# Two attention layers and two FFT convolutions on one core: the residual loaded early, an eight-slot spectrum ring, column-half stores, and twiddles read over dead keys and weights

## The chip, the cores and the metric

The kernel runs on one core of one Trainium2 chip. The metric is the time of one execution in device microseconds (us). Every run below lists its median and, where there were rounds, the ratio to the kernel before, executed in turn with it on the same chip. In the traces, times count from the first instruction of the execution. PE is TensorE, DVE is VectorE, ACT is ScalarE, SP is the engine whose queue issues nearly all transfers (55.46 of the 56.41 MB).

## The reference

Four layers, each added to the residual x: a sliding attention with eight dilated positions, a convolution with a kernel generated from a state-space model and applied by FFT, and both once more.

```python
def _A_ref(x, wqkv, wo):                      # B=1, S=2048, D=512, 32 heads of 16
    W, dil = 8, 2
    q, k, v = split((x @ wqkv))               # cut: reshapes
    idx = pos[:, None] - arange(W)[None, :] * dil      # 8 positions back, step 2
    logits = einsum("bhsd,bhswd->bhsw", q, k[idx]) * Dh ** -0.5   # masked where idx < 0
    return einsum("bhsw,bhswd->bhsd", softmax(logits), v[idx]) @ wo

def _B_ref(u, A, B, C, log_dt, Dskip):        # L=2048, D=512, N=128
    K = einsum("dn,dnl,dn->dl", C, exp(dt * A * l), dt * B).real  # the convolution kernel
    y = irfft(rfft(u, 2L) * rfft(K, 2L))[:L]                      # cut: padding
    return y + u * Dskip

x = A_x
for _ in range(2):
    x = x + _A_ref(layernorm(x), A_wqkv, A_wo)
    x = x + _B_ref(layernorm(x), ...)         # the same weights both times
```

## The kernel before

In an attention core the work goes in this order: for each query block q and feature tile ft, DVE multiplies queries by shifted keys (`prod`), PE sums the products over the features of a head, DVE takes the row maximum (`mx`), ACT the exponentials, DVE normalises. Meanwhile PE makes the v rows. Every four v rows, two copies shift them by one position for the dilated window, and an event may issue other work. Then come sixteen value multiplies (`pav`), each summed by PE and projected, with further events at their places. Engine order is fixed by the program here.

```python
def v_proj(a):
    ...                                                       # cut: matmuls, ACT copy into v
    if a % 4 == 3:                                            # one v block is complete
        b = a // 4
        nc.sync.dma_start(v[1:113, s0:s1, :], v[0:112, s0 + 16:s1 + 16, :])
        nc.sync.dma_start(v[113:128, s0:s1, :], v[112:127, s0 + 16:s1 + 16, :])
        event(("v", b))

for q, ft in slots:
    mult(q, ft); proj(per)                                    # product; projections in between
    if ft == 0 and q > 0: mx(q - 1)
    lsum(q, ft)
    if ft == 0 and q > 0: sub_exp(q - 1)
    if ft == 2 and q > 0: norm_p(q - 1)                       # cut: details
for n in range(16):
    ...; pv_mult(n); ...; event(("p", n)); pv_sum(n)
    if n > 0: out_proj(n - 1)                                 # adds the residual x_sb

ev = {("v", 1): [lambda: k_half_load(0)], ("v", 3): [x_load],
      ("p", 0): [G(gx, 0)], ("p", 1): [G(gw, 0), G(gs, 0), G(gx, 1)], ...,  # inverse twiddle
      ("p", 6): [lambda: k_half_fix(0), K(0, 0)], ("p", 7): [K(0, 1)], ("p", 8): [K(0, 2)],
      ("p", 9): [K(0, 3), lambda: k_half_load(1)], ...}       # kernel rows, in two halves
```

`k_half_load` is 18 small loads of one half of the convolution kernel's rows, in the SP queue; `K(h, j)` copies a quarter of a half into the FFT's order. There is one row buffer, so the second half is loaded only when the first is copied.

The convolution's middle stage (`u_f2`, then `i1`) multiplies each spectrum piece by the kernel's spectrum out of a ring of four slots, and feeds the inverse transform:

```python
def consume(p2, ec):
    kc = self.kf_ring[:, self.nkf % 4]; self.nkf += 1
    for h in range(2):
        nc.sync.dma_start(self.kf_ring[h::2, (self.nkf - 1) % 4], self.kf_dram[g, ec])
    nc.scalar.copy(ub[:], p2...)
    nc.vector.tensor_tensor(t1[...], ub[:], kc[:, 0], ALU.mult)
    nc.vector.tensor_tensor(t2[...], ub[:], kc[:, 1], ALU.mult)
```

## Time and profile before

| | before |
|---|---|
| median of 3 runs | 529.23 us (528.22 to 531.11) |
| span of the profiled run | 525.7 us, granted PE clock 0.933 |
| first product of the first core, first value multiply | 132.72, 171.90 |
| layer norm that closes the first layer (first `ln_bn<-pq`) | 233.46 |
| same for the second layer | 452.22 |
| last convolution's multiply stage, first to last | 467.57 to 500.65 |

A timeline line reads: start, duration, engine, source line, operation, output and inputs, count, and in brackets the idle time just before and what ended it. The prediction below shows the lines of the kernel before that carry it.

### The profile page before, as it was taken

How to read it: one execution, taken by the hardware profiler on the slowest of the kernel's cores; microseconds unless marked ns; L12 is line 12 of the kernel's file. 1: busy time of each engine (PE TensorE's matmuls, PEld its weight loads, DVE VectorE, ACT ScalarE, POOL GpSimd, SP SyncE). 2: the span in 40 equal slices, each digit the busy share in tenths (PEclk: the TensorE clock that was granted, in tenths of full speed). 3: DMA queues.
4: the chain of work that ended last, by engine and by line, in shares of the span. 5: the costliest groups of instructions: out<-in, count | busy, mean ns of one | idle time of the engine just before them, and what ended most of it. 6: DMA issues, size and time to landing. Idle time of an engine off the chain costs nothing.

```text
span 525.7 us, 12773 instructions
## 1 busy us (share of the span) xinstructions
PE 373.4 (71%) x5489; PEld 280.5 (53%) x5528; DVE 421.7 (80%) x570; ACT 330.4 (63%) x529; POOL 44.0 (8%) x56
## 2 busy tenths in 40 slices
PE   1000528899797797888866596889989998695595
PEld 1000225666453665667756485445556776485584
DVE  7799979998796998877679846828999988396843
ACT  5999597764353497788658534674444576695532
POOL 2000131010000002230000000200000013300000
PEclk9999969999797799998989979899998999997889
DMA  8803401011146410328768621161130130218403
GB/s 226 323 1 42 78 1 42 7 22 43 22 119 162 164 42 21 82 88 345 250 205 270 213 82 51 31 247 74 53 90 1 44 120 1 81 52 308 125 2 160
DMA packets 50043, 56.41 MB, mean 107 GB/s; under 512 B 28617, under 2 KB 37962, under 8 KB 48706
## 3 DMA queue, kind: packets, MB, share of 16 engines
q1 hardware_dynamic: 49842, 55.46, 33.1%
q8 instruction: 43, 0.70, 0.6%
q10 hardware_dynamic: 144, 0.13, 0.1%
q14 instruction: 14, 0.11, 0.1%
HBM read 38.67 MB, written 13.24 MB: 99 GB/s over the span
## 4 chain that ended last, share of the span: by engine, by line
PE 37%; DVE 24%; ACT 18%; DMA 7%; issue 6%; SPq 5%; POOL 2%; POOLq 0%; DVEq 0%; ACTq 0%
DVE pav L342 6%; PE pp L201 5%; PE pq L294 4%; PE pq L142 4%; PE pk L961 3%; SPq L1031 3%; PE pb L648 3%; PE pb L698 3%; PE pb L699 3%; PE L L252 3%; PE po L350 2%; DVE t L683 2%; DVE prod L245 2%; DVE t L684 2%; DMA kf_ring<-kf_dram 2%
## 5 line engine op out<-in xcount | busy, mean ns | idle before, releaser
L342 DVE TENSOR_TENSOR pav<-attn,v_ext 128x4096 bf16<-128x4096 bf16 x32 | 72.8, 2282 | 5.3 <-DMA x_sb<-in_A_x_dram 5.3
L350 PE MATMUL po<-ident,pav 128*128 128x128 bf16 x1024 | 64.4, 223 | 15.8 <-DVE pav L342 15.8
L350 PEld LDWEIGHTS <-pav 128*128 128x128 bf16 x1024 | 60.8, 100 | 26.0 <-DVE pav L342 22.9
L245 DVE TENSOR_TENSOR prod<-qT,kT_ext 128x4096 bf16<-128x4096 bf16 x29 | 65.6, 2285 | 5.7 <-PE L L252 4.8
L698 PE MATMUL pb<-Wp,t 128*128 128x128 bf16 x256 | 36.8, 238 | 20.7 <-DVE t L683 18.0
L682 ACT CAST ub<-pb 128x1024 bf16<-128x1024 f32 x32 | 32.1, 1025 | 10.8 <-DVE t L684 9.6
L201 PE MATMUL pp<-xnT,wqk 128*128 128x512 bf16 x123 | 31.9, 397 | 7.8 <-ACT xnT L194 7.1
L698 PEld LDWEIGHTS <-t 128*128 128x128 bf16 x256 | 27.3, 108 | 18.7 <-DVE t L683 18.6
L637 ACT CAST a1s<-pb 128x1024 bf16<-128x1024 f32 x30 | 30.1, 1017 | 10.2 <-PE pb L648 9.2
L296 ACT CAST v_ext<-pq 128x512 bf16<-128x512 f32 x32 | 18.7, 586 | 27.7 <-PE pq L294 27.7
L699 PE MATMUL pb<-WpJ,t 128*128 128x128 bf16 x256 | 35.9, 238 | 0.2 <-DVE t L684 0.2
L192 PE MATMUL pt<-ident,x_blk 128*128 128x128 bf16 x64 | 5.6, 241 | 41.4 <-ACT x_blk L118 41.4
L252 PEld LDWEIGHTS <-prod 128*128 128x128 bf16 x928 | 27.2, 97 | 14.6 <-DVE prod L245 9.4
L657 PE MATMUL pb<-a1s,w_sb 128*128 128x64 bf16 x768 | 30.7, 196 | 6.0 <-DVE a1s L637 2.5
L961 PE MATMUL pk<-B_t,A_t 128*64 128x84 bf16 (+1 forms) x512 | 25.2, 210 | 12.4 <-POOL ln_rstd L100 9.1
L294 PE MATMUL pq<-wv,xnT 128*128 128x512 bf16 x120 | 32.4, 398 | 0.6 <-issue 0.2
L353 ACT CAST oT<-po 128x512 bf16<-128x512 f32 x32 | 18.5, 579 | 22.8 <-PE po L350 22.5
L142 PE MATMUL pq<-xnT,wqk 128*128 128x512 bf16 x118 | 31.3, 391 | 1.6 <-issue 0.8
L252 PE MATMUL L<-ind,prod 128*128 128x8 bf16 x928 | 27.7, 166 | 6.2 <-DVE prod L245 6.0
L100 POOL TENSOR_SCALAR ln_rstd<-ln_veps 128x4 f32<-128x4 f32 (+1 forms) x11 | 15.1, 1370 | 203.1 <-DVE ln_veps L98 203.1
L657 PEld LDWEIGHTS <-w_sb 128*128 128x128 bf16 x768 | 27.1, 100 | 8.8 <-issue 3.9
L961 PEld LDWEIGHTS <-A_t 128*64 128x64 bf16 (+1 forms) x512 | 23.0, 110 | 15.7 <-POOL ln_rstd L100 9.6
(204 smaller groups left out, 913.5 us busy)
## 6 DMA issues: line engine op xcount, KB each, us to landing
kf_ring<-kf_dram SPq DMA_DIRECT2D x64, 256.0 KB
w_sb<-w_dram SPq DMA_DIRECT2D x8, 1024.0 KB
w_dram<-w_zero SPq DMA_DIRECT2D x1, 4096.0 KB
kf_dram<-kf_sb SPq DMA_DIRECT2D x16, 256.0 KB
v_ext<-v_ext SPq DMA_DIRECT2D x6, 448.0 KB
x_blk<-in_A_x_dram SPq DMA_DIRECT2D x4, 512.0 KB
wqk<-in_A_wqkv_dram SPq DMA_DIRECT2D x4, 512.0 KB
x_sb<-in_A_x_dram SPq DMA_DIRECT2D x4, 512.0 KB
```

The lines of the kernel that those rows point to most:

```text
L142: nc.tensor.matmul(pq[:], lhsT=self.wqk[:, dt, ft * P:(ft + 1) * P], rhs=self.xnT[:, dt, q * 512:(q + 1) * 512], start=(dt == 0), stop=(dt ...
L201: nc.tensor.matmul(pp[:], lhsT=self.wqk[:, dt, D + ft * P: D + (ft + 1) * P], rhs=self.xnT[:, dt, b * 512:(b + 1) * 512], start=(dt == 0), ...
L245: nc.vector.tensor_tensor(pr, self.qT[q][:, ft].unsqueeze(1).to_broadcast([P, W, 4, P]), kap, ALU.mult)
L252: self.nc.tensor.matmul(L[:, al, w, ft * 8:(ft + 1) * 8], lhsT=pr[:, w, al, :], rhs=self.c["ind8"][:], start=False, stop=True, skip_group_ ...
L294: nc.tensor.matmul(pp[:], lhsT=xnT[:, dt, a * P:(a + 1) * P], rhs=wv[:, dt, :], start=(dt == 0), stop=(dt == NDT - 1))
L342: nc.vector.tensor_tensor(pv[:], attn[:, n % 4].unsqueeze(2).to_broadcast([P, W, DH, H]), vap, ALU.mult)
L350: nc.tensor.matmul(po[:, ft, :], lhsT=pvf[:, w, ft * P:(ft + 1) * P], rhs=ident[:], start=(w == 0 and ft == 0), stop=(w == W - 1), skip_gr ...
L657: nc.tensor.matmul(p2[:, j, :], lhsT=self.w2[:, ec * EC + j, :], rhs=a1s[:, ec * EC + j, :], start=True, stop=True)
L682: nc.scalar.copy(ub[:], p2[:].rearrange("p e q -> p q e"))
L698: nc.tensor.matmul(p3[:, j, :], lhsT=t1[:, dql, :], rhs=wp_r, start=True, stop=False)
L699: nc.tensor.matmul(p3[:, j, :], lhsT=t2[:, dql, :], rhs=wpj_r, start=False, stop=True)
L961: nc.tensor.matmul(o, lhsT=lhs, rhs=Bt[:, ri, c * CH + ql].rearrange("p b g -> p (b g)"), start=(not half and j % 4 == 0 and ri == 0), sto ...
```

## The change

The intent: take the 18 small loads from in front of the last v shift by issuing them behind it and the residual early; open the pool of products first, so that it doesn't wait for a spare tile; normalise one product later; free space for four more ring slots in the last convolution, by loading the 4 MB forward twiddle over the dead keys and weights; and store the output in column halves, so that half of it leaves a stage sooner.

```diff
-        self.wqk = self.keep.tile([P, NDT, 2 * D], BF16, name="wqk")
-        self.kT = self.keep.tile([P, NDT, NA + 14, P], BF16, name="kT_ext")
+        slot = self.keep.tile([...], BF16, name="kT_ext", tag="slot")   # wqk and kT are views of it
+            self.prp = c2.enter_context(tc.tile_pool(name=f"a{l}_prod", ...))   # now first
             big = c2.enter_context(...)
...
-            self.prp = c2.enter_context(tc.tile_pool(name=f"a{l}_prod", ...))
-                if ft == 2 and q > 0:
+                if ft == 3 and q > 0:
                     norm_p(q - 1)
+    def load_w2(self, w2_dram):
+        w2 = self.keep.tile([P, P * P], BF16, name="w2_sb", tag="slot")
+        ...                                                   # four loads of 1 MB
-        w2p = ... ; self.w2 = w2p.tile(...); 4 x dma_start    # was in FftB.open_mid
+        self.ring2 = (second tile of four slots) if t else None
-            kc = self.kf_ring[:, self.nkf % 4]
+            ring, slot = self.kf_ring[self.nkf // 4 % len(self.kf_ring)], self.nkf % 4
-        ev = {("v", 1): [lambda: k_half_load(0)], ("v", 3): [x_load],
+        ev = {("v", 0): [x_load], ("v", 3): [lambda: k_half_load(0)],
-              ... ("p", 8): [K(0, 2)], ...
+              ... ("p", 8): [lambda: la.load_w2(w2_dram), K(0, 2)], ...
-        la.core(x_sb, u)
+        la.core(x_sb, u, {("p", 8): [lambda: la.load_w2(w2_dram)]})
-    zip_run(fb.i1(1), fb.i2(0, None), lead=2)
-    zip_run(fb.i2(1, <store of 4 full rows>, ("act", "dve")))
+    zip_run(fb.i1(1), fb.i2(0, store(0)), lead=2)             # column half 0 leaves here
+    zip_run(fb.i2(1, store(1), ("act", "dve", "act", "both")))
```

Cut: the pools' closing, and a mask moved into another tile.

More of the change, by code (lines that the diff above doesn't have):

```diff
@@ L129, in __init__ @@
         self.keep = self.ctx.enter_context(tc.tile_pool(name=f"a{layer}_keep", bufs=1, side="right"))
-        self.wqk = self.keep.tile([P, NDT, 2 * D], BF16, name="wqk")
+        slot = self.keep.tile([P, NDT * (2 * D + (NA + 14) * P)], BF16, name="kT_ext", tag="slot")
+        self.wqk = slot[:, 0:NDT * 2 * D].rearrange("p (t c) -> p t c", t=NDT)
         self.wsrc = A_wqkv.rearrange("(dt p) c -> p dt c", p=P)
         self.A_wo = A_wo
-        self.kT = self.keep.tile([P, NDT, NA + 14, P], BF16, name="kT_ext")
+        self.kT = slot[:, NDT * 2 * D:].rearrange("p (t a q) -> p t a q", t=NDT, q=P)
         self.xnT = xnT
@@ L224, in open_logits @@
     def open_logits(self):
-        self.ps_l = self.ctx.enter_context(self.tc.tile_pool(name=f"a{self.layer}_ps_l", bufs=2, space=PSUM, side="right"))
+        self.lctx = ExitStack()
+        self.ps_l = self.lctx.enter_context(self.tc.tile_pool(name=f"a{self.layer}_ps_l", bufs=2, space=PSUM, side="right"))
         self.st = [dict() for _ in range(4)]
@@ L270, in core @@
         with ExitStack() as c2:
+            self.prp = c2.enter_context(tc.tile_pool(name=f"a{l}_prod", bufs=2, reuse_waits="tile"))
             big = c2.enter_context(tc.tile_pool(name=f"a{l}_big", bufs=1, reuse_waits="tile"))
@@ L277, in core @@
             wk = c2.enter_context(tc.tile_pool(name=f"a{l}_wk", bufs=2, reuse_waits="tile"))
-            self.prp = c2.enter_context(tc.tile_pool(name=f"a{l}_prod", bufs=2, reuse_waits="tile"))
             pavp = c2.enter_context(tc.tile_pool(name=f"a{l}_pav", bufs=2, reuse_waits="tile"))
@@ L457, in core, with close_logits @@
             u_apply(14, range(14, 16))
+    def load_w2(self, w2_dram):
+        w2 = self.keep.tile([P, P * P], BF16, name="w2_sb", tag="slot")
+        self.w2 = w2[:].rearrange("p (e c) -> p e c", c=P)
+        for c in range(4):
+            self.nc.sync.dma_start(self.w2[:, c * 32:(c + 1) * 32, :], w2_dram[:, c * 32:(c + 1) * 32, :])
+    def close_logits(self):
+        self.lctx.close()
     def close(self):
@@ L492, in build_b_consts @@
     pf = pk[:, 7:8]
-    aux = cpool.tile([P, 4], F32, name="aux")
+    aux = cpool.tile([P, 8], F32, name="aux")
     nc.vector.tensor_tensor(aux[:, 0:1], pk[:, 6:7], rik, ALU.add)
@@ L497, in build_b_consts @@
     bk, p21 = aux[:, 0:1], aux[:, 1:2]
-    dmask_m = cpool.tile([P, 4], F32, name="dmask_m")
-    nc.vector.tensor_scalar(dmask_m[:], d4i[:], d4m, 2.0 / 4096.0, ALU.is_equal, ALU.mult)
+    dmask_m = aux[:, 4:8]
+    nc.vector.tensor_scalar(dmask_m, d4i[:], d4m, 2.0 / 4096.0, ALU.is_equal, ALU.mult)
     def off_cols(name, rcol, v00, v10, v01, v11):
@@ L555, in build_b_consts @@
         nc.vector.tensor_tensor(w[:], ws[name][:].unsqueeze(2).to_broadcast([P, 32, 4]),
-                                dmask_m[:].unsqueeze(1).to_broadcast([P, 32, 4]), ALU.mult)
+                                dmask_m.unsqueeze(1).to_broadcast([P, 32, 4]), ALU.mult)
         C[name] = w
@@ L614, in open_mid @@
         tc, nc, t = self.tc, self.nc, self.tag
-        w2p = self.c_mid.enter_context(tc.tile_pool(name=f"b{t}_w2", bufs=1, reuse_waits="tile"))
-        self.w2 = w2p.tile([P, P, P], BF16, name="w2_sb")
-        for c in range(4):
-            nc.sync.dma_start(self.w2[:, c * 32:(c + 1) * 32, :], self.w2_dram[:, c * 32:(c + 1) * 32, :])
         nc.sync.dma_start(self.g2[:], self.g2_dram[:])
@@ L622, in open_mid @@
             self.ring_pool = self.c_mid.enter_context(tc.tile_pool(name=f"b{t}_kf", bufs=1, reuse_waits="tile"))
+        self.ring2 = self.c_mid.enter_context(tc.tile_pool(name=f"b{t}_kf2", bufs=1, reuse_waits="tile")) if t else None
         self.nkf = 0
@@ L670, in u_f2 @@
         if self.kf_ring is None:
-            self.kf_ring = self.ring_pool.tile([P, 4, 2, DQG, EC], BF16, name="kf_ring", tag="kp")
+            self.kf_ring = [self.ring_pool.tile([P, 4, 2, DQG, EC], BF16, name="kf_ring", tag="kp")]
+            if self.ring2 is not None:
+                self.kf_ring.append(self.ring2.tile([P, 4, 2, DQG, EC], BF16, name="kf_ring2"))
         t1 = self.gtile("t1", [P, DQG, P])
@@ L676, in consume @@
         def consume(p2, ec):
-            kc = self.kf_ring[:, self.nkf % 4]
+            ring, slot = self.kf_ring[self.nkf // 4 % len(self.kf_ring)], self.nkf % 4
+            kc = ring[:, slot]
             self.nkf += 1
             for h in range(2):
-                nc.sync.dma_start(self.kf_ring[h::2, (self.nkf - 1) % 4], self.kf_dram[g, ec])
+                nc.sync.dma_start(ring[h::2, slot], self.kf_dram[g, ec])
             ub = self.wk.tile([P, DQG, EC], BF16, name="ub")
@@ L714, in i2 @@
                 nc.tensor.matmul(p4[:, j, :], lhsT=self.g2[:, 1, a, :], rhs=z[:, NA + a, :], start=False, stop=True)
-            self.evac(x_sb[:, t * 4:t * 4 + 4, dsl], p4[:], pat[t % len(pat)])
+            if pat[t % len(pat)] == "both":
+                self.evac(x_sb[:, t * 4:t * 4 + 2, dsl], p4[:, 0:2], "act")
+                self.evac(x_sb[:, t * 4 + 2:t * 4 + 4, dsl], p4[:, 2:4], "dve")
+            else:
+                self.evac(x_sb[:, t * 4:t * 4 + 4, dsl], p4[:], pat[t % len(pat)])
             if rows_done is not None:
@@ L1114 @@
         K = lambda h, j: lambda: k_part(h, j)
-        ev = {("v", 1): [lambda: k_half_load(0)], ("v", 3): [x_load],
+        ev = {("v", 0): [x_load], ("v", 3): [lambda: k_half_load(0)],
               ("p", 0): [G(gx, 0)], ("p", 1): [G(gw, 0), G(gs, 0), G(gx, 1)],
               ("p", 3): [G(gw, 1), G(gs, 1), G(gx, 2)], ("p", 4): [G(gw, 2), G(gs, 2), G(gx, 3)], ("p", 5): [G(gw, 3), G(gs, 3)],
-              ("p", 6): [lambda: k_half_fix(0), K(0, 0)], ("p", 7): [K(0, 1)], ("p", 8): [K(0, 2)], ("p", 9): [K(0, 3), lambda: k_half_load(1)],
+              ("p", 6): [lambda: k_half_fix(0), K(0, 0)], ("p", 7): [K(0, 1)], ("p", 8): [lambda: la.load_w2(w2_dram), K(0, 2)], ("p", 9): [K(0, 3), lambda: k_half_load(1)],
               ("p", 12): [lambda: k_half_fix(1), K(1, 0)], ("p", 13): [K(1, 1), K(1, 2)], ("p", 14): [K(1, 3)]}
@@ L1121 @@
     krctx2.close()
-    la.close()
+    la.close_logits()
     z0 = xnT[:].rearrange("p t c -> p (t c)").rearrange("p (m c) -> p m c", m=2 * NA)
     fb = FftB(tc, nc, C, consts["ident"], w2_dram, g2_dram, kf_dram, x_sb, 0)
-    fb.z0, fb.ring_pool = z0, kpp
+    fb.z0, fb.ring_pool, fb.w2 = z0, kpp, la.w2
     fb.open_mid()
@@ L1133 @@
     fb.c_mid.close()
+    la.close()
     la = LayerA(tc, nc, consts, lnst, A_wqkv, A_wo, 1, xnT, 1)
@@ L1150 @@
     with tc.manual_schedule(engines={ET.DVE, ET.Activation, ET.PE, ET.SP}):
-        la.core(x_sb, u)
-    la.close()
+        la.core(x_sb, u, {("p", 8): [lambda: la.load_w2(w2_dram)]})
+    la.close_logits()
     fb = FftB(tc, nc, C, consts["ident"], w2_dram, g2_dram, kf_dram, x_sb, 1)
-    fb.z0, fb.ring_pool = z0, None
+    fb.z0, fb.ring_pool, fb.w2 = z0, None, la.w2
     fb.open_mid()
@@ L1160, with store, rows @@
     fb.c_mid.close()
+    la.close()
     out_v = out.rearrange("b (p a) d -> p (b a) d", p=P)
-    zip_run(fb.i1(1), fb.i2(0, None), lead=2)
-    zip_run(fb.i2(1, lambda t: nc.sync.dma_start(out_v[:, t * 4:(t + 1) * 4, :], x_sb[:, t * 4:(t + 1) * 4, :]), ("act", "dve")))
+    def store(g):
+        gs = slice(g * 4 * DQG, (g + 1) * 4 * DQG)
+        def rows(t):
+            for a in ((t * 4, t * 4 + 2) if (g, t) == (1, 3) else (t * 4,)):
+                a1 = a + (2 if (g, t) == (1, 3) else 4)
+                nc.sync.dma_start(out_v[:, a:a1, gs], x_sb[:, a:a1, gs])
+        return rows
+    zip_run(fb.i1(1), fb.i2(0, store(0)), lead=2)
+    zip_run(fb.i2(1, store(1), ("act", "dve", "act", "both")))
     fb.c_ps.close()
```

## The prediction

> **What bounds the kernel now.** I read the page first, then each engine's timeline around the waits that the change touches, then the queue's timeline. The page says that no engine is the bound for the whole run:
>
> ```profile
> PE 373.4 (71%) x5489; PEld 280.5 (53%) x5528; DVE 421.7 (80%) x570; ACT 330.4 (63%) x529; POOL 44.0 (8%) x56
> ```
>
> DVE carries most, so gaps in DVE that end in something the change removes are what it can win. The first two are in the first attention layer. DVE's timeline (start, duration, and in brackets the idle time before and what ended it):
>
> ```profile
> 128.55 0.71 DVE L210 COPY kT_ext<-kT_ext 128x508 bf16<-128x508 bf16 x1
> 132.72 4.49 DVE L245 TENSOR_TENSOR prod<-qT,kT_ext 128x4096 bf16<-128x4096 bf16 x2 [3.46 <-PE L L252]
> ...
> 165.35 1.22 DVE L307 TENSOR_REDUCE mx<-L 128x128 bf16<-128x1024 f32 x1
> 171.90 4.49 DVE L342 TENSOR_TENSOR pav<-attn,v_ext 128x4096 bf16<-128x4096 bf16 x2 [5.33 <-DMA x_sb<-in_A_x_dram]
> ```
>
> The 5.33 us is blamed on the residual load, but the multiply reads v_ext. The queue in that time shows what it waited for:
>
> ```profile
> 154.54 9.55 SPq L1031 DMA_DIRECT2D k_rl<-kd_dram  x17
> 164.20 0.57 SPq L300 DMA_DIRECT2D v_ext<-v_ext  x1
> 164.82 0.88 SPq L301 DMA_DIRECT2D v_ext<-v_ext  x1
> 165.80 0.87 SPq L300 DMA_DIRECT2D v_ext<-v_ext  x1
> 166.71 0.83 SPq L301 DMA_DIRECT2D v_ext<-v_ext  x1
> 167.58 2.19 SPq L1109 DMA_DIRECT2D x_sb<-in_A_x_dram  x4
> ```
>
> The last v row block left ACT at 162.24 (161.66 + 0.58), yet its two shifting copies are issued only at 165.80, behind 18 small loads of the convolution kernel (0.80 + 9.55 us), and the 2 MB residual then shares the engines with them.
>
> The third place is the last convolution. DVE and the queue:
>
> ```profile
> 477.66 0.68 DVE L684 TENSOR_TENSOR t<-ub,kf_ring 128x1024 bf16<-128x1024 bf16 x1
> 479.90 0.69 DVE L683 TENSOR_TENSOR t<-ub,kf_ring 128x1024 bf16<-128x1024 bf16 x1 [1.56 <-DMA kf_ring<-kf_dram]
> ...
> 485.31 1.23 DVE L637 CAST xnT<-pb 128x1024 bf16<-128x1024 f32 x1 [2.89 <-PE pb L699]
> ...
> 488.39 1.23 DVE L637 CAST xnT<-pb 128x1024 bf16<-128x1024 f32 x1 [0.65 <-PE pb L699]
> ...
> 492.25 1.22 DVE L637 CAST xnT<-pb 128x1024 bf16<-128x1024 f32 x1 [1.44 <-PE pb L699]
> ```
>
> The eighth spectrum multiply waits 1.56 us for its ring slot (four slots), and DVE then idles 2.89 + 0.65 + 1.44 us for inverse-transform tiles that PE could start only after that multiply. After the last tile DVE alone finishes four multiplies while PE waits (PE idle 5.5 us until the multiply of L683).
>
> Fourth, the twiddle loads (4 MB each) and the end:
>
> ```profile
> 232.42 2.04 SPq L618 DMA_DIRECT2D w_sb<-w_dram  x4
> ...
> 517.82 4.26 SPq L1163 DMA_DIRECT2D out_dram<-x_sb  x4
> 520.50 1.22 DVE L637 CAST x_sb<-pb 128x1024 bf16<-128x1024 f32 x1 [1.29 <-PE pb L714]
> ```
>
> [...] from 154 to 164 us the queue issues without a gap (0.56 us each) while the engines average a share of 0.49, 0.18 and 0.54 in the three 4 us windows from 154. [...] PE stops at 163.9, the clock falls from about 165.5; it is 0.50 from 166 to 178 around the first stall and from 480 to 485 after PE's wait in the last convolution. [...]
>
> **The change, part by part.**
>
> *First attention layer.* (a) The pool of products is opened first. In the built program the first product of the core now waits for the last kernel-table matmuls (done at 128.5) and no longer for the L252 sums that read the spare tile in its place. It can start when DVE is free, 128.55 + 0.71 = 129.3 instead of 132.7. PE gains less: its next sums stood idle from 132.7 to 135.07, 2.4 us, and from there PE has no gap over 0.6 us until 164. So the projections, with the last v block, come 2.4 us earlier: ACT finishes it at about 159.8. (b) The normalisation moves one product later; this hides its 1.94 us wait for the exponentials, worth nothing by itself as PE sets the pace here. I stepped DVE through the new order with the two product buffers: the product for block 3 starts when its query arrives (163.1 - 2.4 = 160.7), ends at 162.9, the maximum (1.15) at 164.0. (c) The residual is issued after the first v shift and the kernel loads after the last one, so the last shift is issued at 159.9 and 160.5. In layer 2, where nothing stands in front, the second was issued at 390.37 and landed 3.2 us on (the chain of waits). Here: 163.7, up to 164.5 as the 2 MB residual precedes it. The value multiplies start at 164.0 to 164.5 instead of 171.9: **7.5 us**. From there DVE is nearly full (idle under 1 us in 172 to 200 us), so the gain stays. The kernel loads now run from 161 to 172, well before their first use at 199.8 - 7.5.
>
> *Twiddle over the dead keys, first convolution.* The load moves from 232.4 to about 190 (after the last product, 197.4 - 7.5). At the 426 GB/s seen from 236 to 244 it takes 4.2 MB / 0.426 = 9.8 us, done near 201; the second kernel load starts near 203, so they hardly meet. Its first use, the forward matmuls of L657, is at 245.2, and none of those waited for the load. **0**, perhaps 0.5 less contention.
>
> *Twiddle, second convolution.* It was already loaded at 345.5; now it is at about 417, done at 427, used at 465 in the old clock. **0**. What it buys is space: the rings of the last convolution (8 slots, 16 loads) are filled near 330 to 350, where the queue is free.
>
> *Ring of eight.* All of group 0 is resident, so 1.56 us go. More: the scheduler, seeing no ring wait, now places multiplies 10 and 11 ahead of the first DVE evacuation of the inverse tiles, and leaves two multiplies instead of four for after the last one. I stepped this with the trace's durations (multiply pair 1.20, evacuation 1.14 on DVE; ScalarE 0.92; inverse tile 1.0 us on PE, 1.75 at half clock; four PSUM buffers, three copies). Multiply 8 starts at 478.3. With PE at half clock until about 484, the gaps shrink to 0.95 + 0.6 + 0.45 and the stage ends at 495.8 against 500.65; with a warm PE at 493.8. I take **5.0 us**.
>
> *Stores.* Half of the 2 MB goes out during the stage before, in 512 B rows. The last evacuation is split, but the built program makes the DVE half wait for the ACT half[...]. What remains is the last transfer: 128 KB instead of 512 KB, at 0.4 MB per us 0.33 against 1.28 us (379 and 408 GB/s are seen at the end), less one extra issue of 0.34. **0.6 us.**
>
> Sum: 7.5 + 0 + 0 + 5.0 + 0.6 = 13.1; 529.2 - 13.1 = 516.1, I say 516.
>
> **The rivals.** First, *a new wait takes the place*: the shifts land late behind the residual, since 4 x 512 KB now go ahead of three of the four shifts. The engines ran at 1.0 share with 270 GB/s when they met in the run before. Against it: the residual has 8 us of lead. If the last shift still landed at 167, the first part would be 5 and the total 518.5. Second, *the last convolution is bound by the PE clock, not by the ring*: then only the 1.56 us come off and the total is 519.5. For it: the longest of its gaps (2.89) lies in the half-clock stretch. Against: DVE has multiplies to fill it. Third, *the gain of the first layer is lost to the first convolution*, whose spectrum stores make DVE wait 4.6 us for DMA: this stage follows no fixed clock and only moves along. A mild form, the new order of stores and ring loads, may cost or save 1 us. Fourth, the whole is better than stepped: PE stays warm, 514.
>
> **Range and chances.** The first layer is good to about 1 us, the ring to 2 (1.6 to 7), the rest to 1.5. That gives 511.5 to 521. 2% faster is 518.6; it takes one rival nearly whole to miss it: faster 0.78, same 0.21, slower 0.01.
>
> **What would show it.** In the changed profile: the first product at 129 to 130; the first value multiply near 164 with under 1 us of idle; the queue's v shifts directly after the v rows; no DVE wait for the ring in the last convolution, and its multiply stage under 29 us from first to last (33.1 before); twiddle loads near 190 and 410 without a waiter; a tail from the last matmul of 4.6 us or less (5.2 before). I would be wrong if the first value multiply still waits over 3 us for DMA, if the gaps of the last convolution only change their name, or if a kernel-row fix in the first layer starts to wait for its load.

## The result

The changed kernel took a median of **522.44 us** (520.3 to 523.23, 4 runs) against 528.98 us (528.22 to 531.11, 4 runs): ratio **0.9864** (95% interval 0.9821 to 0.9907). A later run of the same kernel on another chip (after_again, below) gave 0.9793 (0.9742 to 0.9844). A ratio here is the mean time of one kernel's fast runs over that of the other's of the same rounds, so not quite the ratio of the medians quoted. The prediction of 516.0 was too fast by 6.4 us and its range, 511.5 to 521.0, missed the median by 1.4.

The profiled run spans 518.5 us (clock 0.936). No engine's load changed, as the engine line of its page says:

```profile
PE 374.9 (72%) x5489; PEld 283.3 (55%) x5528; DVE 421.4 (81%) x570; ACT 330.0 (64%) x530; POOL 44.1 (9%) x56
```

DVE's timeline of the changed kernel in the first layer, the places shown before:

```profile
128.61 0.72 DVE L211 COPY kT_ext<-kT_ext 128x508 bf16<-128x508 bf16 x1
129.43 4.49 DVE L247 TENSOR_TENSOR prod<-qT,kT_ext 128x4096 bf16<-128x4096 bf16 x2
...
160.68 1.22 DVE L309 TENSOR_REDUCE mx<-L 128x128 bf16<-128x1024 f32 x1
168.38 4.49 DVE L344 TENSOR_TENSOR pav<-attn,v_ext 128x4096 bf16<-128x4096 bf16 x2 [6.48 <-DMA k_rl<-kd_dram]
...
223.14 0.43 DVE L1119 COPY k_perm<-k_rl 128x1024 bf16<-128x1024 bf16 x1 [1.68 <-DMA k_rl<-kd_dram]
...
232.05 0.70 DVE L75 BATCH_NORM_STATS2 ln_bn<-pq 128x6 f32<-128x512 f32 x1 [3.38 <-PE pq L364]
```

The first product comes 3.3 us earlier, and DVE is ready for the value multiplies at 161.9 instead of 166.6. But the wait before them has grown from 5.33 to 6.48 us, and a new wait of 1.68 us stands before a copy of the kernel rows. The queue in the same time:

```profile
151.71 1.96 SPq L1124 DMA_DIRECT2D x_sb<-in_A_x_dram  x4
153.78 0.60 SPq L302 DMA_DIRECT2D v_ext<-v_ext  x1
...
157.53 0.53 SPq L302 DMA_DIRECT2D v_ext<-v_ext  x1
158.10 1.47 SPq L303 DMA_DIRECT2D v_ext<-v_ext  x1
159.61 1.35 SPq L1030 DMA_DIRECT2D k_rl<-kd_dram  x1
162.17 12.81 SPq L1046 DMA_DIRECT2D k_rl<-kd_dram  x17
```

The last shift is issued at 158.1 instead of 166.7, 8.6 us sooner, yet the multiply that reads it starts only 3.5 us sooner. In the last convolution the wait on the ring is gone, and the three gaps before the inverse tiles have shrunk from 2.89 + 0.65 + 1.44 to 0.33 + 0.36 + 0.29:

```profile
482.72 1.23 DVE L645 CAST xnT<-pb 128x1024 bf16<-128x1024 f32 x1 [0.33 <-PE pb L710]
...
485.51 1.22 DVE L645 CAST xnT<-pb 128x1024 bf16<-128x1024 f32 x1 [0.36 <-PE pb L710]
...
488.23 1.23 DVE L645 CAST xnT<-pb 128x1024 bf16<-128x1024 f32 x1 [0.29 <-PE pb L710]
```

To see where the time went I cut every trace at the same seven places of DVE's timeline. A: from the end of DVE's last key copy to the first value multiply. B: to the layer norm that closes the first layer. C: to the last spectrum multiply of the first convolution. D: to the layer norm that closes the second layer. E: to the first spectrum multiply of the last convolution. F: to the end of its last multiply. G: to the end. All in us; the start, some 129 to 131 us, is left out. It is the same work in all of these kernels and differs by up to 1.5 us between executions.

| kernel (fast profiled runs) | A | B | C | D | E | F | G |
|---|---|---|---|---|---|---|---|
| before | 42.6 | 61.6 | 69.4 | 149.3 | 15.4 | 33.1 | 25.1 |
| changed | 39.1 | 63.7 | 68.1 | 150.5 | 16.2 | 27.4 | 24.3 |
| resid_behind | 32.5 | 65.7 | 69.0 | 150.6 | 16.2 | 27.4 | 26.0 |
| krows_behind | 38.5 | 67.0 | 68.4 | 149.9 | 15.2 | 26.2 | 25.6 |
| shifts_alone | 32.5 | 66.4 | 68.5 | 149.9 | 15.2 | 26.2 | 25.6 |
| w2_behind | 41.6 | 62.5 | 68.4 | 149.9 | 15.2 | 26.2 | 25.4 |
| norm_back | 41.3 | 61.9 | 70.5 | 149.3 | 16.1 | 26.2 | 24.6 |
| ring_four | 39.0 | 63.8 | 71.3 | 150.0 | 15.3 | 32.8 | 25.5 |
| pool_back2 | 39.0 | 64.4 | 67.9 | 150.0 | 16.3 | 27.5 | 24.4 |
| before_order | 38.9 | 64.2 | 69.1 | 149.4 | 15.5 | 32.1 | 24.8 |
| rb_sooner | 32.5 | 63.0 | 67.8 | 150.7 | 16.2 | 27.5 | 24.1 |
| rb_gs | 34.3 | 62.8 | 68.3 | 150.0 | 15.3 | 26.2 | 25.7 |
| resid_first | 35.6 | 63.3 | 68.5 | 151.7 | 16.1 | 26.2 | 24.4 |
| joined | 32.5 | 61.6 | 71.0 | 149.3 | 16.1 | 26.2 | 24.5 |
| combo1, the same kernel | 32.5 | 61.4 | 69.0 | 150.7 | 16.3 | 27.5 | 24.2 |

Before to changed: A -3.6, B +2.1, C -1.4, D +1.2, E +0.8, F -5.7, G -0.7; with the start's +0.1 that is the span's -7.2. The first layer, A + B, was to give 7.5 and gave 1.5. C varies by 3.5 us between kernels that do the same there (2.0 between joined and combo1, which are one kernel), E has two values, 15.2 to 15.5 and 16.1 to 16.3, and F and G partly trade against each other (27.4 + 24.3 and 26.2 + 25.5 are the same 51.7; with eight slots the sum runs from 50.6 to 53.4). Differences of that size in one execution are not explained below. A and B trade too: norm_back, whose first layer is the changed kernel's, has A 2.3 longer and B 1.8 shorter than the changed kernel, and no wait on the kernel rows. So a difference of 2 us in B alone means something only where A is equal, and A + B (102.7 and 103.2 in these two) is the safer figure.

### The profile page after: what moved, and what is told of

It reads as the page before. It is cut to its first block, busy times and chain, and to the rows that moved or that the text cites.

```text
span 518.5 us, 12773 instructions
## 1 busy us (share of the span) xinstructions
PE 374.9 (72%) x5489; PEld 283.3 (55%) x5528; DVE 421.4 (81%) x570; ACT 330.0 (64%) x530; POOL 44.1 (9%) x56
## 4 chain that ended last, share of the span: by engine, by line
PE 39%; DVE 22%; ACT 20%; DMA 8%; issue 5%; SPq 3%; POOL 2%; POOLq 0%; DVEq 0%; ACTq 0%
PE pp L202 5%; DVE pav L344 5%; PE po L352 4%; PE pq L143 4%; PE pk L976 3%; PE pb L709 3%; PE pq L296 3%; DMA v_ext<-v_ext 3%; PE pb L710 3%; PE pb L656 3%; PE L L254 3%; DVE prod L247 3%; DMA kf_dram<-kf_sb 2%; DVE t L694 2%; ACT ws L894 2%
## 5 line engine op out<-in xcount | busy, mean ns | idle before, releaser
L352 PE MATMUL po<-ident,pav 128*128 128x128 bf16 x1024 | 67.0, 228 | 14.7 <-DVE pav L344 14.5
L352 PEld LDWEIGHTS <-pav 128*128 128x128 bf16 x1024 | 63.3, 103 | 25.3 <-DVE pav L344 22.1
L202 PE MATMUL pp<-xnT,kT_ext 128*128 128x512 bf16 x123 | 31.9, 396 | 7.7 <-ACT xnT L195 7.0
L693 ACT CAST ub<-pb 128x1024 bf16<-128x1024 f32 x32 | 32.1, 1034 | 6.7 <-DVE t L695 5.9
L355 ACT CAST oT<-po 128x512 bf16<-128x512 f32 x32 | 18.5, 578 | 25.4 <-PE po L352 25.4
L665 PEld LDWEIGHTS <-w_sb 128*128 128x128 bf16 x768 | 28.3, 102 | 9.1 <-DVE a1s L645 3.9
L143 PE MATMUL pq<-xnT,kT_ext 128*128 128x512 bf16 x118 | 31.3, 392 | 1.6 <-issue 0.8
L364 PE MATMUL pq<-wop,oT 128*128 128x512 bf16 x112 | 29.7, 379 | 2.5 <-ACT oT L355 1.7
L254 PE MATMUL L<-ind,prod 128*128 128x8 bf16 x928 | 27.5, 166 | 4.9 <-DVE prod L247 4.7
```

Source lines behind the costliest of these rows:

```text
L143: nc.tensor.matmul(pq[:], lhsT=self.wqk[:, dt, ft * P:(ft + 1) * P], rhs=self.xnT[:, dt, q * 512:(q + 1) * 512], start=(dt == 0), stop=(dt ...
L202: nc.tensor.matmul(pp[:], lhsT=self.wqk[:, dt, D + ft * P: D + (ft + 1) * P], rhs=self.xnT[:, dt, b * 512:(b + 1) * 512], start=(dt == 0), ...
L254: self.nc.tensor.matmul(L[:, al, w, ft * 8:(ft + 1) * 8], lhsT=pr[:, w, al, :], rhs=self.c["ind8"][:], start=False, stop=True, skip_group_ ...
L352: nc.tensor.matmul(po[:, ft, :], lhsT=pvf[:, w, ft * P:(ft + 1) * P], rhs=ident[:], start=(w == 0 and ft == 0), stop=(w == W - 1), skip_gr ...
L665: nc.tensor.matmul(p2[:, j, :], lhsT=self.w2[:, ec * EC + j, :], rhs=a1s[:, ec * EC + j, :], start=True, stop=True)
L693: nc.scalar.copy(ub[:], p2[:].rearrange("p e q -> p q e"))
```

## The experiments

**Theory A**: the last shifts of v are late because the residual's 2 MB stand ahead of them on the transfer engines. **Rival B**: the 18 small loads issued right behind the last shift slow it. **Rival C**: the layer is paced by something else. The four runs shared one chip (before: median 532.33).

### resid_behind: the residual behind the last shift

```diff
-        ev = {("v", 0): [x_load], ("v", 3): [lambda: k_half_load(0)],
+        ev = {("v", 3): [x_load, lambda: k_half_load(0)],
```

> The changed kernel with one move: the residual's four loads (2 MB) are issued behind the last shift of v instead of behind the first. Theory A (the residual, queued ahead of the last three shifts, holds them up): the last shift is issued near 156.5 instead of 158.1, the first value multiply starts at 162 to 163.5 instead of 168.4, without the 6.48 us wait, and the layer norm that ends the first layer comes 5 us earlier (near 227); time near 517.5. Rival B (the 18 small loads of kernel rows issued right behind the last shift slow it): the first value multiply stays within 1 us of 168.4 and the time within 1 us of the changed kernel's 522.4. Rival C (the first layer is held later by something else): the first value multiply starts near 162.5, but the layer norm stays later than 230.

Measured: 517.71 us, ratio **0.970** (0.9616 to 0.9784). DVE's timeline, then the queue's:

```profile
161.31 1.22 DVE L309 TENSOR_REDUCE mx<-L 128x128 bf16<-128x1024 f32 x1
162.45 4.48 DVE L344 TENSOR_TENSOR pav<-attn,v_ext 128x4096 bf16<-128x4096 bf16 x2
```

```profile
158.74 0.82 SPq L303 DMA_DIRECT2D v_ext<-v_ext  x1
159.60 2.28 SPq L1124 DMA_DIRECT2D x_sb<-in_A_x_dram  x4
161.92 1.18 SPq L1030 DMA_DIRECT2D k_rl<-kd_dram  x1
163.15 12.69 SPq L1046 DMA_DIRECT2D k_rl<-kd_dram  x17
```

The last shift is issued later than in the changed kernel (158.74 against 158.10), and the multiply starts 5.9 us earlier, with no wait at all: the shift landed within 3.7 us of its issue, not in 10.3. A fell by 6.6 us. Theory A holds, B does not: the small loads are still right behind. The stretches of 4 us (busy time of PE, its loads, DVE, ACT, POOL; PE clock; mean share of the transfer engines; GB/s) show what the shift met, first in the changed kernel, then here:

```profile
154.00:158.00 4.00, 4.00 (x63) 2.46 (x62) 3.86 (x6) 1.98 (x4) 0.00 (x0) 1.00 1.04 343
158.00:162.00 4.00, 2.06 (x56) 1.48 (x54) 3.89 (x3) 0.36 (x1) 0.00 (x0) 0.98 0.98 281
162.00:166.00 4.00, 2.44 (x5) 0.64 (x5) 0.00 (x0) 2.32 (x4) 0.00 (x0) 0.59 1.02 252
```

```profile
154.00:158.00 4.00, 3.95 (x51) 2.23 (x49) 3.70 (x5) 1.62 (x3) 0.00 (x0) 1.00 0.79 229
158.00:162.00 4.00, 2.24 (x58) 1.60 (x57) 3.97 (x4) 0.73 (x2) 0.00 (x0) 1.00 0.67 158
```

In the changed kernel the engines are full from 154 to 166 and move 4 x (343 + 281 + 252) = 3,500 KB, nearly all of it the residual and the shifts. The shift has left the issuing queue at 159.6, and the multiply that reads it starts at 168.4; in between, to 166, the share of the engines is 0.98 and 1.02. With the 2 MB ahead of it the shift took 10.3 us from issue to use, with the same 2 MB behind it at most 3.7: in these two runs it paid for what was queued ahead of it.

But B grew to 65.7 us, so A + B is 98.2 in place of 104.2, a gain of 6.0. The layer norm at 228.14 is 3.9 us earlier than the changed kernel's, not the 5 expected, so a part of rival C is true: something holds the layer later. Two waits of DVE are new or large, one for indices from ACT and one for the kernel rows; ACT itself had waited 3.06 us for a store of the inverse twiddle:

```profile
179.92 1.06 ACT L589 ACTIVATE g_s<-g_i 128x1024 bf16<-128x1024 int32 x1 [3.06 <-DMA g_dram<-g_s]
187.10 0.69 DVE L585 TENSOR_SCALAR g_i<-g_i 128x1024 int32<-128x1024 int32 x1 [1.78 <-ACT g_i L582]
...
219.23 0.43 DVE L1119 COPY k_perm<-k_rl 128x1024 bf16<-128x1024 bf16 x1 [1.61 <-DMA k_rl<-kd_dram]
```

### krows_behind: the small loads moved away instead

```diff
                                                              # cut: the lines replaced
+        ev = {("v", 0): [x_load],
+              ("p", 1): [G(gw, 0), G(gs, 0), lambda: k_half_load(0), G(gx, 1)],
```

> The changed kernel with one move: the first half of the kernel rows (18 small loads) is issued behind the first store of the inverse twiddle, near 178, instead of right behind the last shift of v. The residual stays where the change puts it. Theory A (residual ahead): the first value multiply stays at 167 to 168.4; time 522. Rival B (small loads behind the shift): it starts near 162 to 163.5, time near 517.5. Either way the copies of the first half must not wait: the load lands near 191 and is used at 196.

Measured: 524.52 us, ratio 0.9865 (0.9801 to 0.993). DVE:

```profile
168.05 4.49 DVE L344 TENSOR_TENSOR pav<-attn,v_ext 128x4096 bf16<-128x4096 bf16 x2 [5.92 <-DMA v_ext<-v_ext]
```

The wait stays with nothing behind the shift, and it is now put down to the shift itself. Rival B is refuted. No small load was issued between 159.2 and 177.6, and the page still has the engines at 220 GB/s in its slice from 156.1 to 169.1 (the changed kernel, whose loads are issued from 159.6 on: 244 from 155.6 to 168.5). B rose to 67.0, as the loads now stand ahead of the inverse twiddle's stores in the one queue (a DVE wait of 3.96 us for ACT's indices).

### shifts_alone: both moves

```diff
                                                              # cut: the lines replaced
+        ev = {("v", 3): [x_load],
+              ("p", 1): [G(gw, 0), G(gs, 0), lambda: k_half_load(0), G(gx, 1)],
```

> The changed kernel with both moves: residual behind the last shift of v, kernel rows behind the first store of the inverse twiddle. It is the most that a clear queue can give here: the first value multiply at 162, when the row maxima are done (161.9), so 6.4 us earlier than the changed kernel; time 516.5 if this is kept to the end of the first layer. Theory A says this is no faster than the residual's move alone (within 0.7 us), rival B says no faster than the kernel rows' move alone.

Measured: 515.97 us, ratio 0.9722 (0.9659 to 0.9784). A is 32.5, as with the residual's move alone (32.49 and 32.50): moving the small loads adds nothing there. The times of the two do not differ by more than their spread.

### w2_behind: the first layer's twiddle behind the kernel rows

```diff
-  ("p", 8): [lambda: la.load_w2(w2_dram), K(0, 2)], ("p", 9): [K(0, 3), lambda: k_half_load(1)],
+  ("p", 8): [K(0, 2)], ("p", 9): [K(0, 3), lambda: k_half_load(1), lambda: la.load_w2(w2_dram)],
```

> The changed kernel with one move: the first layer's twiddle load (4 MB) is issued behind the second half of the kernel rows instead of 13 us ahead of them. Theory D (the early twiddle costs the end of the first layer some 2 us: copies wait on it, the matmuls at 196 run at half clock, and the kernel rows' second half is issued only 2 us earlier than before): no idle time on the twiddle near 200, kernel rows issued near 207.5 instead of 209.0, layer norm at the end of the layer near 230.5 instead of 232.05; the twiddle, issued near 217.5, lands near 230, ahead of its first use near 243; time 521. Rival E (the twiddle is not the cause, or moves its load on to the spectrum's stores): the layer norm stays at 232 and the time at 522.4 or above.

Measured: 521.47 us, ratio 0.9798 (0.9737 to 0.9859), not to be told from the changed kernel's 0.9864 and 0.9793. In the trace B is 62.5, 1.1 less, and the wait on the rows is 0.47 in place of 1.68. But A was 2.5 us longer in this execution, so the layer norm came at 234.82, not at the 230.5 of theory D; and norm_back below, with the twiddle where the change puts it, has a B of 61.9 and no wait on the rows at all. The idle time of 0.24 us that the changed kernel's trace puts down to the twiddle stands here too (0.23 at 204.34, put down to the layer norm). So theory D isn't shown, by trace or time, and it isn't refuted either.

The next four ran on a second chip (before: 530.95).

### norm_back: the second layer's normalisation put back

```diff
-                if ft == 3 and q > 0:
+                if ft == (2 if l else 3) and q > 0:
```

> The changed kernel with the normalisation of the second layer put back to where it was (after the third product of a query block, not the fourth); the first layer keeps the new place. Theory G (the late normalisation costs the second layer: DVE runs three products in a row and then waits 0.78 us for PE to free a product buffer): that wait goes, the span from the layer's third product (357.44 in the changed kernel) to its closing layer norm (450.62) shrinks from 93.2 to between 91.7 and 92.4 us (before it was 91.7, from 360.52 to 452.22), time 0.8 to 1.5 us less, so near 521.3. Rival: the loss comes from the last shift of v landing 0.51 us late, and the span stays at 93 or more.

Measured: 521.82 us, ratio 0.9825 (0.9763 to 0.9886). In DVE's timeline of the changed kernel this line stands in the second layer:

```profile
371.43 2.29 DVE L247 TENSOR_TENSOR prod<-qT,kT_ext 128x4096 bf16<-128x4096 bf16 x1 [0.78 <-PE L L254]
```

The wait stands in every fast trace with the late normalisation and is gone here. The span that the expectation speaks of is 91.71 us (361.09 to 452.80), as before (91.70). Theory G holds in the trace; the two runs of the joined kernel, which has this line too, give 91.71 and 91.70. The line that moves the normalisation is shared by both layers; in the second it only costs, 0.8 us, and another 0.5 to 0.6 where the last shift then came late. The time cannot show so little.

### ring_four: four slots in the last convolution

```diff
-  self.ring2 = <second ring tile> if t else None
+  self.ring2 = None
```

> The changed kernel with four ring slots in the last convolution, as before, and everything else of the change. Theory (the ring of eight is worth what was predicted, 5.0 us, and the trace of the changed kernel shows 5.7): the multiply stage takes 32 to 33 us from its first to its last multiply in place of 27.4, with a wait of 1 to 2 us on the ring; time near 527.5. Rival (TensorE's clock decides the stage, and the ring gives only its own wait): stage 29 us, time near 524.

Measured: 527.31 us, ratio 0.9928 (0.986 to 0.9996). F is 32.8 in place of 27.4. DVE's timeline:

```profile
481.60 0.69 DVE L694 TENSOR_TENSOR t<-ub,kf_ring 128x1024 bf16<-128x1024 bf16 x1 [1.00 <-DMA kf_ring<-kf_dram]
...
486.80 1.22 DVE L645 CAST xnT<-pb 128x1024 bf16<-128x1024 f32 x1 [2.63 <-PE pb L710]
...
493.62 1.22 DVE L645 CAST xnT<-pb 128x1024 bf16<-128x1024 f32 x1 [1.68 <-PE pb L710]
```

The ring's wait is only 1.0, but the gaps before the inverse tiles come back with it. The eight slots are worth 5.4 us (6.6 with G, since F and G trade); the rival, the PE clock, would have left a stage of 29. The changed kernel's trace speaks against the clock too: it is 0.50 from 478 to 482 there as well (before: 0.50 from 480 to 485), and the gaps are still only 0.29 to 0.36.

### pool_back and pool_back2: the pool of products opened last again

```diff
-            self.prp = c2.enter_context(...)       # ahead of `big`
+            self.prp = c2.enter_context(...)       # behind `wk`, as before
```

> The changed kernel with the pool of products opened last again, so that the first product waits for the sums that read the spare tile. The first product then starts near 132.7 instead of 129.4. Theory A' (the first value multiply is set by the transfer of residual and shifts, not by when DVE and PE get there): the last shift is issued some 2 us later, near 160, and lands near 169 to 170; the first value multiply starts 1 to 2 us later than 168.4 and the time grows by 1 to 2 us only. If the 3.3 us of the pool order count in full: first value multiply at 171.5, time near 525.7. If not at all: 168.4 and 522.4.

The profiled execution of the first run took 1261.65 us; matmuls of 512 columns (L202) took 1.10 us instead of 0.40, while the recorded clock said 1.000. Nothing explains it; it is set aside. Its time is not in the ratio. The other three took 519.72 to 521.73, ratio 0.9814 (0.9761 to 0.9868). So I ran it again, with five rounds, on a third chip (before: 530.04), together with the changed kernel word for word.

> The same kernel as in the earlier run with the pool of products opened last, whose profiled execution fell in a disturbed state (1261.65 us, all matmuls some 2.8 times as long) while its other three took 519.7 to 521.7. Theory A' in its strong form, after those times: the 3.3 us at the first product are lost in full in the wait before the first value multiply: first product near 132.7, first value multiply within 1 us of the changed kernel's 168.4, ratio within 0.003 of the changed kernel's on this chip. Rival: first value multiply near 170 or later, ratio 0.003 to 0.006 higher.

Measured: 521.07 us, ratio 0.9834 (0.979 to 0.9877); the changed kernel beside it 520.43 us (519.90 for its four fast runs), 0.9793 (0.9742 to 0.9844). DVE's timeline of pool_back2:

```profile
133.90 4.50 DVE L247 TENSOR_TENSOR prod<-qT,kT_ext 128x4096 bf16<-128x4096 bf16 x2 [3.46 <-PE L L254]
...
169.40 4.49 DVE L344 TENSOR_TENSOR pav<-attn,v_ext 128x4096 bf16<-128x4096 bf16 x2 [1.32 <-DMA k_rl<-kd_dram]
```

The wait of 3.46 us before the first product is back, and the wait before the first value multiply is shorter by 5.2 us: A is 39.0 with and without the pool's new place. In the changed kernel the wait behind the residual takes the whole gain of the pool order at this place. In time the expectation was missed by a little: the ratio is 0.0041 higher, not within 0.003, which is in the rival's range; and 169.40 is 1.02 us past 168.4, in an execution that started this stage 1.1 later. Whether the 0.004 is real is left open, as the intervals overlap.

> The changed kernel, word for word, on the chip of the three runs beside it, so that they can be compared with it. Expected ratio to the kernel before 0.982 to 0.991, as measured with the prediction (0.9864).

Its profiled execution counted as slow (two of six were, over 1.5% above its fastest), so its trace isn't used. The median of 520.43 is over all six.

### before_order: the order alone, in the kernel before

```diff
-        ev = {("v", 1): [lambda: k_half_load(0)], ("v", 3): [x_load],
+        ev = {("v", 3): [x_load, lambda: k_half_load(0)],
```

> The kernel before with one move alone: residual and first half of the kernel rows issued behind the last shift of v, in this order. Theory A: the last shift is issued near 162.5 and lands before DVE is ready (166.57), so the first value multiply starts at 166.6 instead of 171.9: 5.3 us at that place; what the layer keeps of it is limited by the one queue (the stores of the inverse twiddle and the second half of the rows stand behind the 18 small loads), so that 3 to 5 us remain at its closing layer norm (233.46 before); time 524 to 526, ratio 0.991 to 0.994. Rival (the small loads behind it slow the shift as much as those ahead of it): 170 or later and a ratio above 0.997.

Measured: 529.5 us, ratio 1.0014 (0.9962 to 1.0066): a miss in time. In the trace the wait of 5.33 us is gone and A fell by 3.8 us, though the first product started 1.7 us later in its stage than before (a wait of 5.12 in place of 3.46). From the first product to the first value multiply it is 33.7 us in place of 39.2, the 5.3 expected. But B grew by 2.6, to 64.2. What is left, 1.2 us of A + B or 2.8 counted from the first product, was not found in the time (the interval allows 1.2). A clear path for the shift is worth little while the rest of the layer gives it back.

### rb_sooner, rb_gs and joined: what gives it back

Two moves on top of resid_behind, apart and together. The first copies the kernel rows one step sooner and loads the second half ahead of the twiddle; the second issues the inverse twiddle's stores from ACT's queue, so that they don't stand behind the 18 loads.

```diff
 rb_sooner:                                                   # cut: the lines replaced
+  ("p", 5): [G(gw, 3), G(gs, 3), lambda: k_half_fix(0), K(0, 0)],
+  ("p", 6): [K(0, 1)], ("p", 7): [K(0, 2)],
+  ("p", 8): [K(0, 3), lambda: k_half_load(1), lambda: la.load_w2(w2_dram)],
 rb_gs:
-        nc.sync.dma_start(g2_dram[:, :, h * 4:(h + 1) * 4, :], gs[:])
+        nc.scalar.dma_start(g2_dram[:, :, h * 4:(h + 1) * 4, :], gs[:])
 joined (combo1 is the same kernel): both, and norm_back's line
```

> The changed kernel with the residual behind the last shift of v and the copies of the kernel rows one step sooner, so that the rows' second half is loaded sooner and ahead of the twiddle; the stores of the inverse twiddle stay in the one queue, the second layer's normalisation as changed. It parts the remedies of the joined run. From the first value multiply to the closing layer norm that run took 61.4 to 61.6 us, the run with the residual's move alone 65.7. If the late second half of the rows and the early twiddle are the cause: 62 to 63 us, with the wait on the rows (1.61) gone but the one on the sines' indices (1.78) still there. If the stores in the one queue are the cause: 64 to 65. Time 514 to 516.5.

Measured: 513.39 us, ratio 0.9707 (0.9631 to 0.9783); this and the next ran on the second chip again (before in these rounds: 529.31). B is 63.0, the wait on the rows is gone, the one on the indices (1.77) stands, as expected.

> The changed kernel with the residual behind the last shift of v and the stores of the inverse twiddle issued from ScalarE's queue; nothing else. If the stores in the one queue are the cause of the slow second half: the wait on the sines' indices (1.78 us) goes, 63.5 to 64 us from the first value multiply to the layer norm, the wait on the kernel rows (1.6) stays. If they are not: 65 to 66. Time 515 to 517.5.

Measured: 514.24 us, ratio 0.9728 (0.9659 to 0.9798). B is 62.8, better than expected: the wait on the indices fell from 1.78 to 1.03, and the wait on the rows is gone. But A was 1.8 us longer in this execution, and norm_back shows that a late start alone can take the wait on the rows away. A + B is 1.1 us less than in resid_behind, or 2.0 counted from the first product. For rb_sooner, with A equal, B gives 2.7.

> The changed kernel with the residual behind the last shift of v, the stores of the inverse twiddle issued from ScalarE's queue, the copies of the kernel rows one step sooner, the second half of the kernel rows ahead of the first layer's twiddle, and the second layer's normalisation as before. If the loss in the second half of the first layer comes from the one queue (18 small loads of 0.56 us each in front of the stores, and the second half of the rows issued late): from the first value multiply to the closing layer norm 61.5 to 62.5 us, as before (61.56), instead of 65.7 in the run with the residual's move alone; no wait of the copies on kernel rows; closing layer norm near 224.5; total 512 to 513.5. Rival (something else paces the layer once it starts sooner, for instance ScalarE): 64 us or more there, total 516 to 517.

Measured: 512.40 us, ratio **0.9658** (0.9609 to 0.9707), on the second chip. B is 61.4: what the layer had before. A is as in rb_sooner, so the stores' move adds 1.4 to 1.6 us of B to that run's 2.7. This is read in traces; the ratios of resid_behind, rb_sooner and rb_gs (0.970, 0.9707, 0.9728) can't be told apart, and resid_behind's interval overlaps that of the joined kernel. Timed once more with five rounds beside the changed kernel:

> The same kernel as the run that joined the remedies (512.4 us, ratio 0.9658), timed once more beside the changed kernel on one chip: ratio to before 0.963 to 0.969, and 1.7 to 2.3% below the changed kernel.

Measured: 512.29 us (510.43 to 513.56, 6 runs), ratio **0.9667** (0.9634 to 0.9701) against 0.9793 for the changed kernel on the same chip. By these it is 1 - 0.9667 / 0.9793 = 1.3% below the changed kernel (1.5% by the medians of the fast runs, 512.29 and 519.90), less than the 1.7 to 2.3% that I expected. DVE's timeline:

```profile
161.98 4.49 DVE L344 TENSOR_TENSOR pav<-attn,v_ext 128x4096 bf16<-128x4096 bf16 x2
...
223.60 0.70 DVE L75 BATCH_NORM_STATS2 ln_bn<-pq 128x6 f32<-128x512 f32 x1 [3.28 <-PE pq L364]
```

The layer closes at 223.60, 9.9 us before the kernel before and 8.5 before the changed one. In time it beats both.

### resid_first: the residual earlier still

```diff
-        ev = {("v", 0): [x_load], ("v", 3): [lambda: k_half_load(0)],
+        x_load()                                    # ahead of la.core
+        ev = {("v", 3): [lambda: k_half_load(0)],
```

> The changed kernel with the residual issued ahead of the first attention layer instead of behind the first shift of v; the scheduler puts its four loads among and behind the stores of the kernel table, between about 131 and 148. If bytes in flight beside the shifts are the cause (theory A), the 2 MB are in by 155 and the last shift lands in time: first value multiply 32.5 to 34 us after DVE's last key copy, as with the residual behind (32.5; the changed kernel 39.05). If it is the queue's outstanding loads that hold up the shifts, rather than the bytes, 34 to 37. If it delays the kernel table or the weights, the first product comes over 1 us later. Time 516 to 518.

Measured: 518.07 us, ratio 0.9783 (0.9719 to 0.9847). A is 35.6, between the two, and so in the range that the expectation gave to the queue's outstanding loads, not to the bytes. The run doesn't separate them: only one of the four loads left early, at 129.82, and the other three between 146.47 and 149.27, not long before the changed kernel's 151.71; the first shift is issued at 153.8 where resid_behind had 150.8, and the engines are full (share 0.99) from 154 to 158. That the 2 MB ahead cause the wait is shown by resid_behind. In the changed kernel the full engines from 154 to 166 speak for the bytes, but no run excludes the other way. The first product is not delayed. Earlier helps by half; behind is better, since nothing needs the residual before the first output projection.

## Why the prediction was wrong

**The step that failed** is in (c) of the first layer: "Here: 163.7, up to 164.5 as the 2 MB residual precedes it." All that leads to it held or came better: first product 129.43 (129.3 said), last v block on ACT 157.5 (159.8), last shift issued at 158.1 (160.5), DVE ready at 161.9 (164.0). The landing was 168.4. The 3.2 us from issue to landing had been read off the second layer, where the share of the engines was 0.28 from 388 to 392 and 0.18 from 392 to 396, and only up to 0.8 was added for 2 MB ahead. The prediction had the numbers to see it: 2 MB and three shifts of some 0.5 MB make 3.6 MB, and at the 270 GB/s that it quotes for such a meeting that is an estimate of 13 us from 152, so 165 and a landing on top. Its first rival named this very wait and set its cost at 2.5 us; with the multiply at 168.4 it was about 4. Of its own three signs of being wrong, one came outright, as the first value multiply waits over 3 us for DMA (6.48), and one nearly: not the fix of the kernel rows but the copy behind it waits for the load (1.68).

**The second failed step**: "so the gain stays". The queue's timeline was read for the shifts but not for what else goes through it. B grew by 2.1 us in the changed kernel, 1.68 of it the wait on the rows' second half (in norm_back the same layer has A longer and B 0.3 above before: of the 7.5, A + B kept 1.5 and 1.0). It grew by 4.1 as soon as the multiplies started earlier still, because then the stores of the inverse twiddle, behind 18 loads in one queue, also hold up ACT and through it DVE (in resid_behind the loads were issued until 175.84 and the first store at 175.95; ACT waited 3.06 us for it, DVE 1.78 for ACT's indices); in the changed kernel itself no one waits for them. The joined run shows that these two are the cause of the 4.1: with both moved, B is 61.4 to 61.6 again, and A + B gives 10.1 us, more than the 7.5 hoped for.

**A smaller one**: the later normalisation, "worth nothing by itself", costs the second layer 0.8 us, since both layers share the line of code.

**What was right.** The ring: 5.0 said, 5.7 in the trace, 5.4 by ring_four, and the last convolution's wait at the ring gone. The stores: 0.6 said; from the last evacuation's end to the end of the span 3.98 us before (521.72 to 525.7) and 3.25 after (515.25 to 518.5), though the split's DVE half waits for the ACT half as foreseen (0.59 and 0.69 us). The twiddles: near 0. The load at 194.3 came 4 us after the time given; whether it slows the rows' second half is open (w2_behind); the one in the second layer (415.6) kept no one waiting. With the first layer's term corrected from 7.5 to 1.5 the sum is 7.1, and 529.2 - 7.1 = 522.1; 522.44 was measured. That it fits so well is partly luck: C, D and E differ by -1.4, +1.2 and +0.8, unforeseen and cancelling, and F and G together gave 6.4 where 5.6 was said. As for the chances, "same", given 0.21, came out at the first measurement, and the interval of the second straddles 2%.

## What to carry to other kernels

A latency read where the transfer engines have little to do (3.2 us at shares of 0.18 to 0.28) must not be carried to a place where megabytes are queued ahead (10.3 us here, behind 2 MB): count the bytes issued before a small urgent transfer, and put the bulk behind it if no one needs it first. When a wait is taken away, list everything else that goes through the same issuing queue until the layer ends: in resid_behind B grew by 4.1 us at items that kept their old place. A change of order in code that two layers share must be stepped through in both.

## Also measured

- In the changed kernel issue took longer where the engines were full. The 17 small loads of the rows' first half took 12.81 us to issue, from 162.17: the first five 5.9 us, with the share of the engines at 1.02 from 162 to 166, the other twelve 6.9 us. The 17 of the second half took 9.62 us from 209.68, at shares of 0.22 and 0.27 from 210 to 218.
- The same idle time of PE came with two clocks. In the changed kernel PE idled 1.25 us before its matmuls at 196.09, and the clock from 196 to 198 was 0.50. In the kernel before it idled 1.25 us before the same matmuls, at 199.61, and the clock from 198 to 202 was 1.00. Around its 1.62 us of idle before 165.49 the clock was 1.00 up to 165 and 0.50 from 165.5 to 178. So these traces show no one length of idle from which the clock falls.
